# Two score halves of the first attention block held back for VectorE's copies, and a cap of four key tiles on the block behind it

## The chip, the cores and the metric

The kernel runs on one NeuronCore of one Trainium2 chip. The metric is the device time of one execution in microseconds. Before the change it is 1393.85 us, the median of three runs (1393.54 to 1394.19).

## The reference

One layer on 2048 tokens of 512 features, all in float32. Cut to what matters:

```python
xn = _layernorm(x)
# attention, 32 heads of 16
qkv = (xn @ wqkv).reshape(B, S, 3, 32, 16)...
scores = einsum("bhqd,bhkd->bhqk", q, k) * 16 ** -0.5
s = einsum("bhqk,bhkd->bhqd", softmax(scores), v) ... @ wo
# feed-forward of the same xn, hidden width 1792
f = (silu(xn @ w_gate) * (xn @ w_up)) @ w_down
return x + s * silu(f)
```

## The kernel before, in words

**Engines.** PE (TensorE) does every matmul, ACT (ScalarE) the exponentials and the tanh, DVE (VectorE) copies, casts and splits, POOL (GpSimd) a few fills and element-wise products, and SP issues most DMAs. Each engine runs its own instructions in the order in which the program wrote them. They wait for each other by semaphores, when a buffer has to be full or has to be free.

**Stages.** A prologue (up to about 156 us) normalises the tokens and projects queries, keys and values to DRAM. Then comes the attention, with the feed-forward and the output projection dealt out between its matmuls, and a short tail.

**Attention.** Its work is cut into 32 units (8 groups of four heads, times 4 blocks of 512 queries). A unit has 16 key tiles of 128 keys. The key tiles of a unit are grouped into *blocks* of 2 to 6 tiles, written `(k, n)` below: k key tiles, and n slots of other work. `plan()` (L62 to L115) makes the list of blocks. A key tile has two *pairs* of score matmuls (L906), and a pair is two matmuls (h = 0 and 1) which sit in different row groups of the array and run side by side. The pairs of a block are numbered n = 0 to 2k - 1 (the loop at L885). After pair n come `parts[n]` fills (`fill`, L924). A fill is one step of the feed-forward generator `ffn` (L251), which is two matmuls side by side as well (L242). So a pair and a fill cost PE one *slot* each.

**Banks.** Each score half takes one PSUM bank of 512 floats. Even pairs go to the two banks of `score`, and one 1024-wide exponential (L909) empties both. Odd pairs go to `single0` and `single1`, each emptied by a 512-wide exponential (L916). The last pair of a block goes to `single0` and to the bank `spare`. A bank is free for its next pair when its reader has finished. In the rows that follow buffer numbers are mostly left out, so `single` is either of the two.

**Halves kept back.** Where a pair's number stands in the block's `shared` list (L902, L912), one of its halves is not read by ACT: DVE copies it to SBUF (L913), which frees the bank, and ACT does its exponential there in place (L926) when all pairs and fills of the block have been issued. An even pair in that list uses `spare` for its second half.

**Values.** The value matmuls of a block (`values`, L423, matmul L428, all of the array, no fill beside them) are issued inside the next block, ahead of its pair n = 2. So pairs n = 0 and n = 1 of a block run before the values of the block ahead of it.

**What the planner does.** `plan()` fixes the first block by hand (4 tiles, no shared halves, fills from `FIRST`) and searches the rest for the cheapest way through key tiles and fills: each block costs 327 plus terms for bad shapes (L92). Block shapes that stand in `SHARED` have lists made by hand. `FIRST[0]` fills are issued ahead of the first block (L881), and `FIRST[1:]` are the fills behind its eight pairs.

**Other work that the opening carries.** After every 24 fills one hidden tile is complete: ACT does a tanh (`th`, L269), and DVE two products (`ga`, L270 and L271) and splits into a high and a low part (`hh`, L235 and L236). At the first fill of each hidden tile DVE splits the gate and up weights of a later one (`guh` and `gul`, L203 and L204). At the 24th fill of the first tile in the attention and at the 8th fill of the later ones DVE splits a down weight (`wd`, L213 and L214). There is one buffer for the raw down weight (`wdr`), and its next load (L209, on SP) starts when the split has read it. POOL writes rows of ones into two key buffers (L160) shortly after the attention has begun.

Before the change the list of blocks begins (4, 20), (6, 24), (6, 24), with 4 fills ahead of it.

Of the kernel before, what the change touches and what calls it, by code (L numbers as in the profile page):

```python
# [40 lines left out]
LIMIT = 160.0  # L41
SIZES = (2, 3, 4, 5, 6)
LAST = (3, 3, 3, 3, 2, 2)
FIRST = (4, 1, 4, 0, 4, 1, 2, 4, 4)
EARLY = 2


# [14 lines left out]
def plan():  # L62

    ends = [0]
    for i in range(2 * NB):  # L70
        nf = GROUPS[i % 2].stop - GROUPS[i % 2].start
        for n in [3 * DC] * nf + [3 * nf] * NT:
            ends.append(ends[-1] + n)

    ends = [n - ends[1] for n in ends[2:]]
    first = [(4, ends[0])]
    units = H // 4 * NB
    start, stop = sum(k for k, _ in first), (units - 2) * KT
    pace = (ends[-1] - ends[0]) / (stop - start)
    short = lambda k, n: 60 if (k, n) in SHARED else 250 * max(0, 6 * (k - 1) - n)  # L80
    ways = {at: {} for at in range(start, stop + 1)}
    ways[start][ends[0], 4] = 0, None
    for at in range(start, stop):
        room = KT - at % KT
        for (done, last), (cost, _) in ways[at].items():
            rem = next((n for n in ends if n > done), done) - done
            for k in SIZES:
                for n in [rem] + list(range(3, rem - 2)):
                    to = at + k, done + n
                    if not n or n > 6 * k + 6 or k > room or room - k == 1:  # L90
                        continue
                    if abs(to[1] - ends[0] - (to[0] - start) * pace) > 45:  # L92
                        continue
                    c = cost + 327 + short(k, n) + (120 if k == 6 and n < 24 else 0) + (700 if k == last == 6 and n < 24 else 0) + (650 if n == rem and k == 2 else 0) + abs(n - 4.1 * k) / 2
                    if (to[1], k) not in ways[to[0]] or ways[to[0]][to[1], k][0] > c:
                        ways[to[0]][to[1], k] = c, ((at, (done, last)), (k, n))

    rest = [3 * (DT - 1)] * EARLY
    pairs = {4: (2, 2), 5: (3, 2), 6: (3, 3)}
    best = lambda r: min((w[0], key) for key, w in ways[stop - r].items() if key[0] == ends[-1])  # L100
    cost = lambda r: best(r)[0] + sum(short(k, n) for k, n in zip(pairs[r], rest))
    r = min((r for r in pairs if any(done == ends[-1] for done, _ in ways[stop - r])), key=cost)
    middle, step = [], ways[stop - r][best(r)[1]][1]
    while step:
        middle.insert(0, step[1])
        step = ways[step[0][0]][step[0][1]][1]
    rest += [3 * DT] * (NT * (NB - 1))
    parts = []
    for k, n in first + middle + list(zip(pairs[r] + 2 * LAST, rest)):
        m = 2 * k - 2  # L110
        even = [n // m + (i < n % m) for i in range(m)]
        shared, behind = SHARED.get((k, n), ((), even))
        parts.append((k, shared, [0, 0, *behind]))
    parts[0] = 4, (), list(FIRST[1:])
    return parts  # L115


# [1 line left out]
def tile_block(ctx: ExitStack, tc: tile.TileContext, x, wqkv, wo, w_gate, w_up, w_down, out):  # L119
# [356 lines left out]
    def fill(n):  # L476
        nonlocal given
        while n > 0 and not blocked():
            next(queue[0][1])
            queue[0][2] -= 1  # L480
            if not queue[0][2]:
                queue.pop(0)
            n -= 1
            given += 1

    blocks = plan()

    begin, n = [], 0
# [381 lines left out]
    for u in range(units):  # L870
# [3 lines left out]
        for now in range(begin[u], begin[u + 1]):  # L874
# [5 lines left out]
            if not now:  # L880
                fill(FIRST[0])  # L881
            if now < 2:
# [140 lines left out]
```

## Time and profile before

| what | us |
|---|---|
| median of three runs | 1393.85 |
| the profiled execution | 1393.63 |
| its span, first to last instruction | 1391.9 |
| attention's first slot to the fourth block's pair n = 2 | 156.15 to 198.53 |
| PE busy, of the span | 1383.6 |
| ACT busy, of the span | 1155.7 |
| DVE busy, of the span | 772.5 |

The granted TensorE clock is 0.999 over the span. In a timeline a row has the start in us, the duration in us, the engine, the line, the operation with output and inputs, the shape and the number of instructions merged, and in brackets the idle time of the engine ahead of it with what ended it. PEld is PE's loading of weights, which runs ahead of the matmul that uses them, and which waits where the matmul's bank is not free yet.

### The profile page before, as it was taken

The page shows a single profiled execution, that of the slowest core. Times are in us where ns is not written, and L with a number is a line of the kernel's source. Part 1 is how long each engine was busy: PE and PEld are TensorE (multiplying, and loading weights), DVE is VectorE, ACT ScalarE, POOL GpSimd, SP SyncE. Part 2 cuts the span into 40 slices and gives each one's busy share as a digit, 9 for nine tenths or more (in the row PEclk, how much of TensorE's full clock was granted, in tenths as well). Part 3 has the DMA queues.
Part 4 walks back from the last instruction along what each step waited for, and adds up shares of the span by engine and source line. Part 5 has one row for each costly group of instructions (what it writes and reads, how often), then busy time and mean ns, then how long its engine had stood idle before and what let it go on. Part 6 is the DMA issues. An engine that isn't in the chain of part 4 may idle for free.

```text
span 1391.9 us, 27666 instructions
## 1 busy us (share of the span) xinstructions
PE 1383.6 (99%) x11197; PEld 863.9 (62%) x11197; DVE 772.5 (56%) x1242; ACT 1155.7 (83%) x1932; POOL 89.4 (6%) x102
## 2 busy tenths in 40 slices
PE   9999999999999999999999999999999999999998
PEld 7788656556555655665556555666556556655554
DVE  6643466355646664565465643665466445655755
ACT  6733588888989898889998988888989888899874
POOL 4200100000000000000000000000000000000344
PEclk9999999999999999999999999999999999999999
DMA  7778541124463511233723402357323311232543
GB/s 241 263 249 269 141 116 44 35 69 112 98 138 81 134 43 36 50 87 87 170 60 109 114 13 51 74 127 152 84 67 94 99 28 47 73 102 85 190 146 108
DMA packets 128693, 149.21 MB, mean 107 GB/s; under 512 B 12593, under 2 KB 80689, under 8 KB 127790
## 3 DMA queue, kind: packets, MB, share of 16 engines
q1 hardware_dynamic: 123246, 126.72, 35.5%
q0 software_dynamic: 4880, 20.12, 3.9%
q8 instruction: 90, 1.47, 0.5%
q10 hardware_dynamic: 432, 0.52, 0.1%
q14 instruction: 45, 0.37, 0.1%
HBM read 107.46 MB, written 40.11 MB: 106 GB/s over the span
## 4 chain that ended last, share of the span: by engine, by line
PE 86%; DVE 2%; ACT 1%; issue 0%; DVEq 0%
PE acc L428 32%; PE bankx L242 29%; PE score L906 9%; PE single L906 8%; PE banky L242 6%; PE spare L906 1%; ACT pr L916 0%; ACT pr L909 0%; PE spare L961 0%; PE banky L961 0%; DVE pr L913 0%; DVE gul L204 0%; DVE wd L335 0%; DVE wd L334 0%; DVE on L446 0%
## 5 line engine op out<-in xcount | busy, mean ns | idle before, releaser
L428 PE MATMUL acc<-pr,vst 128*17 128x512 f32 x4096 | 460.4, 593 | 0.0
L916 ACT ACTIVATE pr<-single 128x512 f32<-128x512 f32 x759 | 427.7, 605 | 19.9 <-PE spare L906 3.1
L909 ACT ACTIVATE pr<-score 128x1024 f32<-128x1024 f32 x327 | 337.1, 1031 | 90.3 <-PE score L906 86.7
L242 PE MATMUL bankx<-fx,guh 64*128 64x512 f32 x896 | 290.3, 392 | 0.1
L242 PE MATMUL banky<-fx,guh 64*128 64x512 f32 x896 | 290.4, 392 | 0.0
L428 PEld LDWEIGHTS acc<-pr,vst 128*17 128x17 f32 x4096 | 114.9, 97 | 277.9 <-issue 273.6
L913 DVE COPY pr<-spare 128x512 f32<-128x512 f32 x185 | 127.9, 691 | 169.0 <-PE spare L906 156.8
L906 PE MATMUL score<-qst,kst 50*128 50x512 f32 x839 | 218.9, 419 | 0.0
L906 PE MATMUL single<-qst,kst 50*128 50x512 f32 x916 | 212.9, 399 | 0.8 <-DVE pr L913 0.7
L242 PE MATMUL banky<-wd,hh 64*128 64x512 f32 x672 | 196.1, 392 | 0.0
L242 PE MATMUL bankx<-wd,hh 64*128 64x512 f32 x672 | 196.0, 391 | 0.0
L926 ACT ACTIVATE pr<-pr 128x512 f32<-128x512 f32 x342 | 187.2, 641 | 1.3 <-DVE pr L913 1.3
L242 PEld LDWEIGHTS bankx<-fx,guh 64*128 64x128 f32 x896 | 166.8, 186 | 21.3 <-DVEq L815 0.6
L242 PE MATMUL bankx<-fx,gul 64*128 64x512 f32 x448 | 175.8, 392 | 0.0
L242 PE MATMUL banky<-fx,gul 64*128 64x512 f32 x448 | 175.5, 392 | 0.0
L906 PEld LDWEIGHTS score<-qst,kst 50*128 50x128 f32 x839 | 98.2, 184 | 118.4 <-ACT pr L916 77.1
L242 PEld LDWEIGHTS banky<-fx,guh 64*128 64x128 f32 x896 | 166.9, 186 | 2.0
L913 DVE COPY pr<-single 128x512 f32<-128x512 f32 x157 | 108.4, 691 | 64.8 <-PE single L906 36.9
L916 ACT ACTIVATE pr<-score 128x512 f32<-128x512 f32 x185 | 111.4, 602 | 34.9 <-PE spare L906 27.5
L242 PEld LDWEIGHTS bankx<-wd,hh 64*128 64x128 f32 x672 | 125.1, 186 | 18.9
L906 PEld LDWEIGHTS single<-qst,kst 50*128 50x128 f32 x916 | 114.0, 184 | 26.5 <-ACT pr L916 8.3
L242 PEld LDWEIGHTS banky<-wd,hh 64*128 64x128 f32 x672 | 125.1, 186 | 5.2
(179 smaller groups left out, 1680.3 us busy)
## 6 DMA issues: line engine op xcount, KB each, us to landing
gur<-in_B_w_gate_dram SPq DMA_DIRECT2D x56, 256.0 KB
gur<-in_B_w_up_dram SPq DMA_DIRECT2D x56, 256.0 KB
wdr<-in_B_w_down_dram SPq DMA_DIRECT2D x56, 256.0 KB
kst<-k_d SPq DMA_DIRECT2D x192, 64.0 KB
qst<-q_d SPq DMA_DIRECT2D x192, 64.0 KB
fx<-xt_d SPq DMA_DIRECT2D x24, 512.0 KB
q_d<-parts SPq DMA_DIRECT2D x16, 512.0 KB
k_d<-parts SPq DMA_DIRECT2D x16, 512.0 KB
```

The source lines that it names most:

```text
L242: mm(bank, lhs[h], rhs[h], start=start, stop=stop)
L428: mm(acc[h * 32:h * 32 + DH + 1], v[:, kt % CT, h * (DH + 1):(h + 1) * (DH + 1)], probs[2 * i + h // 2][:, h % 2], start=kt == 0, stop=kt ...
L906: mm(banked[h], k[r, j, kc * P:(kc + 1) * P], q[r, j], start=True, stop=True)
L909: exps.append(act(pr, both_banks, AF.Exp, scale=0.25))
L913: dve.tensor_copy(pr[:, h], banked[h])
L916: exps.append(act(pr[:, h], banked[h], AF.Exp, scale=0.25))
L926: exps.append(act(part, part, AF.Exp, scale=0.25))
```

## The change

Three edits, all in `plan()` and its tables. `FIRST` deals the 24 fills of the opening otherwise: 2 in place of 4 ahead of it, and 2, 4, 1, 3, 4, 2, 2, 4 behind its pairs in place of 1, 4, 0, 4, 1, 2, 4, 4. `OPEN` gives the first block a `shared` list of pairs 5 and 7. And a block that follows the first one costs 900 more if it has over four key tiles.

```diff
-FIRST = (4, 1, 4, 0, 4, 1, 2, 4, 4)
+FIRST = (2, 2, 4, 1, 3, 4, 2, 2, 4)
+OPEN = (5, 7)
...
-                    c = cost + 327 + short(k, n) + ... + (700 if k == last == 6 and n < 24 else 0) + (650 if n == rem and k == 2 else 0) + abs(n - 4.1 * k) / 2
+                    c = cost + 327 + short(k, n) + ... + (700 if k == last == 6 and n < 24 else 0) + (900 if at == start and k > 4 else 0) + (650 if n == rem and k == 2 else 0) + abs(n - 4.1 * k) / 2
...
-    parts[0] = 4, (), list(FIRST[1:])
+    parts[0] = 4, OPEN, list(FIRST[1:])
```

The list of blocks then begins (4, 22), (2, 9), (4, 15), (6, 24), with 2 fills ahead of it. From the block that starts at key tile 10 of the first unit on, it is the list of before, block for block, one place later (109 blocks in place of 108). Lines behind the tables have a number higher by one.

What moves on DVE, from the start of the attention on. Before (`gur` are the raw gate and up weights, `pr` a tile of probabilities):

```order
L203 CAST guh<-gur 128x1024
L204 TENSOR_TENSOR gul<-gur,guh 128x1024
L270 SCALAR_TENSOR_TENSOR ga<-th,bankx 128x512
L271 SCALAR_TENSOR_TENSOR ga<-ga,banky 128x512
L235 CAST hh<-ga 128x512
```

And now, at the same place:

```order
L204 CAST guh<-gur 128x1024
L205 TENSOR_TENSOR gul<-gur,guh 128x1024
L914 COPY pr<-single_8968 128x512
L914 COPY pr<-single_8967 128x512
L271 SCALAR_TENSOR_TENSOR ga<-th,bankx 128x512
L272 SCALAR_TENSOR_TENSOR ga<-ga,banky 128x512
L236 CAST hh<-ga 128x512
```

Two copies of score halves now stand ahead of the first hidden tile's products, where there was none.

Further on, on DVE behind the split of the first down weight, before:

```order
L203 CAST guh<-gur 128x1024
L204 TENSOR_TENSOR gul<-gur,guh 128x1024
L913 COPY pr<-spare 128x512
L213 CAST wd<-wdr 128x512
L214 TENSOR_TENSOR wd<-wdr,wd 128x512
L913 COPY pr<-spare 128x512
L913 COPY pr<-single_8968 128x512
L913 COPY pr<-spare 128x512
L913 COPY pr<-single_8968 128x512
L270 SCALAR_TENSOR_TENSOR ga<-th,bankx 128x512
```

And now:

```order
L204 CAST guh<-gur 128x1024
L205 TENSOR_TENSOR gul<-gur,guh 128x1024
L214 CAST wd<-wdr 128x512
L215 TENSOR_TENSOR wd<-wdr,wd 128x512
L914 COPY pr<-spare 128x512
L914 COPY pr<-single_8968 128x512
L914 COPY pr<-single_8967 128x512
L271 SCALAR_TENSOR_TENSOR ga<-th,bankx 128x512
```

The five copies of the old second block are gone from among the weight splits. The second block has none now, and the three copies here are those of the new third block, all behind the split of the second down weight.

On ACT, from the opening block's pair n = 4 on, before (`score` is the pair of banks that one exponential empties):

```order
L909 ACTIVATE pr<-score_8966 128x1024
L916 ACTIVATE pr<-single_8967 128x512
L916 ACTIVATE pr<-single_8968 128x512
L909 ACTIVATE pr<-score_8966 128x1024
L916 ACTIVATE pr<-single_8967 128x512
L916 ACTIVATE pr<-spare 128x512
L269 ACTIVATE th<-bankx 128x512
L909 ACTIVATE pr<-score_8966 128x1024
```

And now, from the same pair on:

```order
L910 ACTIVATE pr<-score_8966 128x1024
L917 ACTIVATE pr<-single_8967 128x512
L910 ACTIVATE pr<-score_8966 128x1024
L917 ACTIVATE pr<-spare 128x512
L270 ACTIVATE th<-bankx 128x512
L927 ACTIVATE pr<-pr 128x512 x2
L910 ACTIVATE pr<-score_8966 128x1024
```

Two of ACT's exponentials out of PSUM became two in SBUF, and stand behind the tanh, still ahead of the second block's first one. On SP the DMAs stand in the order of before.

More of the change, by code (lines that the diff above doesn't have):

```diff
@@ L93, in plan @@
                         continue
-                    c = cost + 327 + short(k, n) + (120 if k == 6 and n < 24 else 0) + (700 if k == last == 6 and n < 24 else 0) + (650 if n == rem and k == 2 else 0) + abs(n - 4.1 * k) / 2
+                    c = cost + 327 + short(k, n) + (120 if k == 6 and n < 24 else 0) + (700 if k == last == 6 and n < 24 else 0) + (900 if at == start and k > 4 else 0) + (650 if n == rem and k == 2 else 0) + abs(n - 4.1 * k) / 2
                     if (to[1], k) not in ways[to[0]] or ways[to[0]][to[1], k][0] > c:
```

## The prediction, made before the changed kernel was run

> **What bounds the kernel now.** I read the page's first part, then the opening by stages.
>
> ```profile
> PE 1383.6 (99%) x11197; PEld 863.9 (62%) x11197; DVE 772.5 (56%) x1242; ACT 1155.7 (83%) x1932; POOL 89.4 (6%) x102
> ```
>
> PE is busy for 99% of the span, ACT for 83%. So only time that PE loses can be won. The change reaches the first ten key tiles, and from there on the list of blocks is the old one. So I cut the stretch from the first slot (156.15) to the fourth block's pair n = 2 (198.53) where the value matmuls begin and end. Columns: length, then busy time (instructions) of PE, PEld, DVE, ACT and POOL, the clock, DMA.
>
> ```profile
> 156.15:165.54 9.39, 9.39 (x69) 6.84 (x69) 1.44 (x2) 8.35 (x14) 3.78 (x4) 1.00 0.75 173
> 165.54:169.10 3.56, 3.56 (x35) 0.84 (x34) 3.01 (x6) 2.21 (x4) 0.00 (x0) 1.00 0.02 5
> 169.10:179.16 10.06, 9.31 (x77) 7.22 (x73) 7.67 (x12) 7.87 (x14) 0.00 (x0) 1.00 0.57 146
> 179.16:184.43 5.27, 5.27 (x50) 1.39 (x48) 4.32 (x6) 4.97 (x10) 0.00 (x0) 1.00 0.72 178
> 184.43:193.26 8.83, 8.83 (x76) 7.58 (x73) 4.48 (x7) 7.87 (x14) 0.00 (x0) 1.00 0.47 105
> 193.26:198.53 5.27, 5.27 (x50) 1.39 (x48) 4.54 (x7) 4.97 (x10) 0.00 (x0) 1.00 0.02 4
> ```
>
> The rows are: slots of block 0 (and n = 0, 1 of block 1), its values, slots of block 1, its values, slots of block 2, its values; 42.38 us together. What these slots cost without a wait is read from the same shapes later:
>
> ```profile
> 285.16:293.83 8.67, 8.67 (x76) 7.02 (x73) 3.41 (x5) 7.78 (x14) 0.00 (x0) 1.00 0.33 77
> 293.83:299.11 5.28, 5.28 (x52) 1.39 (x50) 4.32 (x6) 4.98 (x10) 0.00 (x0) 1.00 0.00 0
> 1279.67:1285.21 5.54, 5.54 (x50) 4.21 (x46) 2.44 (x4) 4.80 (x9) 0.00 (x0) 1.00 0.26 74
> 1288.77:1291.99 3.22, 3.22 (x30) 2.38 (x27) 1.04 (x2) 2.39 (x5) 0.54 (x1) 1.00 0.97 354
> 1291.99:1293.83 1.84, 1.84 (x18) 0.37 (x17) 1.70 (x4) 1.84 (x3) 0.00 (x0) 1.00 1.03 383
> ```
>
> They are a (6, 24) block, its values, a (4, 15) block, a (2, 9) block, its values; four tiles' values take 3.56, as above. Block 1, a (6, 24), takes 10.06 against 8.67, so it loses **1.39**; block 2 loses **0.16**. Block 0 has 8 pairs, 24 fills and two pairs of block 1, 34 slots. The first score pair, and the first and the last start of four undisturbed slots:
>
> ```profile
> 157.15 0.44 PE L906 MATMUL score<-qst,kst 50*128 50x512 f32 x2
> ...
> 162.88 0.39 PE L242 MATMUL banky<-fx,guh 64*128 64x512 f32 x1
> ...
> 163.81 0.40 PE L906 MATMUL spare<-qst,kst 50*128 50x512 f32 x1
> ```
>
> From 162.88 to 163.81, four slots in 0.93 make 0.2335 each, and 34 make 7.94, with 0.10 ahead of the values 8.04. Block 0 takes 9.39, so it loses **1.35**. Where these losses are, PEld's timeline shows, by who ended its wait:
>
> ```profile
> 159.23 0.18 PEld L906 LDWEIGHTS single<-qst,kst 50*128 50x128 f32 x1 [0.30 <-ACT pr L916]
> 162.54 0.19 PEld L906 LDWEIGHTS score<-qst,kst 50*128 50x128 f32 x2 [0.39 <-ACT pr L909]
> 173.19 0.18 PEld L906 LDWEIGHTS spare<-qst,kst 50*128 50x128 f32 x1 [0.55 <-DVE pr L913]
> 175.46 0.18 PEld L906 LDWEIGHTS spare<-qst,kst 50*128 50x128 f32 x1 [1.05 <-issue]
> ```
>
> In block 0 the banks come back late from ACT. In block 1 they come back late from DVE's copies of `spare`, 0.55 and 1.05 (the row names the issue, but a copy that is shown below ends at 175.39, just ahead of it). The Trainium skill (Trainium Kernel Development and Optimization, Performance Expectations) holds matmul busy time for a bad measure, since matmuls are pipelined, and takes LDWEIGHTS instead. By PE's busy time the six windows hide no more than 0.75 (10.06 less 9.31), and the sum below would be a gain of at most 0.75. By the spacing of the slots they hide 2.90. The trace sides with the page: the rows of PEld show waits in the first window, where PE counts as busy throughout.
>
> **Block 0.** The two halves kept back are two DVE copies, and two exponentials that read SBUF in place of PSUM. Their prices, and ACT's queue in the opening:
>
> ```profile
> L916 ACT ACTIVATE pr<-single 128x512 f32<-128x512 f32 x759 | 427.7, 605 | 19.9 <-PE spare L906 3.1
> L926 ACT ACTIVATE pr<-pr 128x512 f32<-128x512 f32 x342 | 187.2, 641 | 1.3 <-DVE pr L913 1.3
> 157.67 1.03 ACT L909 ACTIVATE pr<-score 128x1024 f32<-128x1024 f32 x1 [1.04 <-DVE gul L204]
> 158.59 1.08 ACT L916 ACTIVATE pr<-single 128x512 f32<-128x512 f32 x2
> 159.55 1.04 ACT L909 ACTIVATE pr<-score 128x1024 f32<-128x1024 f32 x1
> ...
> 166.60 1.15 ACT L916 ACTIVATE pr<-single 128x512 f32<-128x512 f32 x2
> 169.64 1.03 ACT L909 ACTIVATE pr<-score 128x1024 f32<-128x1024 f32 x1 [1.89 <-PE score L906]
> ```
>
> ACT starts 0.52 after the first score pair (157.15), and then runs without a break until 167.75: 0.92 for a full pair, 0.96 for two halves. Then it sits idle for 1.89 while PE does the values. The halves kept back move 2 x 0.5 us from the full stretch into this idle time, and cost there 2 x 0.04 more than out of PSUM.
>
> The walk: with 2 fills ahead, n = 0 goes to PE at 156.15 + 0.53 = 156.68, its exponential runs from 157.20 to 158.23, those of n = 1 end at 158.72 and 159.20. PE wants n = 3 ten slots after n = 0, at 159.02: its second bank is free at 159.24, a wait of 0.23. n = 4 would go at 160.0; the exponential of n = 2 (159.09 to 160.12) frees it at 160.17 with the release, a wait of 0.12 with what the first left. n = 5 wants the banks of n = 3 (free at 161.1) at 161.35; n = 6 those of n = 4 (162.05) at 162.05; n = 7 half of n = 5 (162.5) at 162.75, and `spare`, which nobody used. Block 1's n = 1 wants DVE's copy of n = 7 (163.9) at 164.15. So 0.33 of 1.35 stays, and the values begin at 164.5: **gain 1.02**. The same walk over the list of before puts them at 165.50, where the trace has 165.54. The bounds: 1.35 (no wait left) and, where copies and exponentials run later than walked, nothing or a loss (rival B).
>
> The copies cost nothing by this: DVE is idle ahead of 165.88 for 8.26, and two copies of 0.69 take 1.38 of it.
>
> ```profile
> 165.88 0.69 DVE L270 SCALAR_TENSOR_TENSOR ga<-th,bankx 128x512 f32<-128x512 f32 x1 [8.26 <-ACT th L269]
> 169.98 0.69 DVE L214 TENSOR_TENSOR wd<-wdr,wd 128x512 fp32r<-128x512 f32 x1
> 170.70 0.36 SPq L209 DMA_DIRECT2D wdr<-in_B_w_down_dram x1
> 172.45 0.68 DVE L913 COPY pr<-spare 128x512 f32<-128x512 f32 x1
> 173.64 0.43 DVE L213 CAST wd<-wdr 128x512 fp32r<-128x512 f32 x1 [0.50 <-DMA wdr<-in_B_w_down_dram]
> 174.71 0.68 DVE L913 COPY pr<-spare 128x512 f32<-128x512 f32 x1
> ```
>
> **Blocks 1 and 2.** From 165.88 on DVE works off the first hidden tile and the weight splits, without a break until 173.1. The copies of the old block 1 queue behind that, and then behind the second down weight, whose load leaves SP at 170.70 and lands at 173.64, 2.94 later. The new block 1 has no copies, so nothing that PE needs stands behind the splits: its cost is that of the (2, 9) block above, and the loss of **1.39** goes. What is late next is block 2's copy of n = 2. The tanh comes 1.0 earlier, so the first down weight is split by 169.65, the second one lands at about 172.6 and is split by 173.75, and the copy can begin with its score, done at about 173.75. It ends at 174.45, and PE wants `spare` again for n = 7, at about 177.0: **2.5 us of slack**. The three halves of block 2 kept back cost ACT 3 x 0.64 beside 3.56 of values. The (6, 24) behind it is the old block 2; I take its **0.16** for a rest of the same backlog, which goes too.
>
> The price of one more block: from the windows, (2, 9) and (4, 15) take 3.22 + 1.84 + 5.54 + 3.56 = 14.16, the (6, 24) in whose place they stand 8.67 + 5.28 = 13.95, so **0.21** more. Score, value and fill matmuls are as many as before. DMAs stand in their old order on SP; keys and queries are loaded well ahead.
>
> **Sum:** -1.02 - 1.39 - 0.16 + 0.21 = -2.36. The profiled execution takes 1393.63 (1.73 more than its span), and would take 1391.27. It is 0.22 under the median, so 1393.85 - 2.36 = 1391.49.
>
> **Rivals.**
>
> A, the forecast: 1391.2 to 1391.8.
>
> B, GpSimd holds the copies up. The new copies meet POOL's four fills, and a DVE operation next to POOL has taken longer elsewhere:
>
> ```profile
> 34.98 1.30 POOL L555 TENSOR_TENSOR wl<-wraw,wh 128x512 fp32r<-128x512 f32 x1 [1.98 <-ACT wh L551]
> 35.02 1.54 DVE L611 TENSOR_SCALAR xn<-facc,mv,rs 128x512 f32<-128x512 f32 x1
> 45.63 3.90 POOL L160 MEMSET kst<- 2x1024 f32 x4
> 45.65 0.69 DVE L702 TENSOR_TENSOR parts<-ps,parts 128x512 fp32r<-128x512 f32 x1 [0.84 <-ACT parts L701]
> 160.74 3.94 POOL L160 MEMSET kst<- 2x1024 f32 x4 [11.33 <-ACT pr L909]
> ```
>
> The scaling out of SBUF took 1.54 beside a POOL subtraction of 1.30. A DVE subtraction out of PSUM took 0.69 beside the same four fills, and the copies out of PSUM above take 0.68 each. If each new copy waits out one fill (0.98), block 1's n = 1 goes 0.4 later: 1391.9. If both wait for the last fill (164.7), its bank is free at 165.4 and block 0 loses 2.0 more: 1393.5. The Trainium skill (SBUF — State Buffer, Who interferes with whom) calls the port pair that VectorE and GpSimd share an exclusive lock: whoever comes second blocks fully. It exempts operations with one SBUF input at most outside the two-port modes, and the subtraction's 0.69 agrees; no row shows a copy out of PSUM beside POOL.
>
> C, the change does half of what it says: block 1's loss comes back in the two short blocks, because DVE is busy there for 7.67 (window 169.10:179.16) where the (2, 9) and (4, 15) windows had 1.04 and 2.44. Without 1.39 of the gain: 1392.9. Against it stands the slack of 2.5.
>
> D, slower. Block 2's only use of `spare` ahead of n = 7 stands on DVE behind the split of the second down weight. A landing later than 2.94 + 2.5 = 5.4 after its issue delays PE one to one; from 7.8 on the kernel is slower than before, and at 11 it is 0.2% slower (1397). The row shows 2.94, and the old block 1 felt only 0.50 of it.
>
> E, more than forecast: block 0 without any wait, and runs at the low end (they spread by 0.3 around the median): 1390.9.
>
> **How the numbers follow.** A measurement of this kernel can tell about 0.2% from no change, which is 2.8 us: faster means under 1391.06. Chances: A 0.76, B 0.08 (0.05 and 0.03), C 0.07, D 0.03, E 0.06. So the likeliest is faster by 0.17%, within that bound. E and a little of A make faster 0.07, D's far end slower 0.02, the rest 0.91. The range takes in A, B's near case, C and E: 1390.9 to 1392.9.
>
> **What would show it.** The first value matmul at about 164.5; block 0's values follow at once with no wait for the two late exponentials; slots of about 3.2 and 5.5 in blocks 1 and 2; the (6, 24) block's pair n = 2 at about 182.2 in place of 184.43; copies of 0.69 beside the fills. Wrong are the steps if a copy takes over 1 us (B), or if PEld waits for DVE in block 1 or 2 (C, D).

## The result: 1.90 us faster, 0.14%, and the profile after

The changed kernel takes 1391.99 us, the median of 22 runs (1391.70 to 1392.22). The kernel before, run beside it, takes 1393.89 (22 runs, 1393.28 to 1394.67). The ratio is 0.9987, with a 95% interval of 0.9981 to 0.9993. That is a gain of 1.90 us. It lies inside the 0.2% that the prediction counts as no change, though the interval lies clear of 1, and it is 0.46 less than the 2.36 of the forecast. The profiled execution takes 1391.74, its span is 1389.9. This is the engines' line of its page:

```profile
PE 1382.6 (99%) x11197; PEld 867.1 (62%) x11197; DVE 772.6 (56%) x1242; ACT 1155.8 (83%) x1930; POOL 89.6 (6%) x102
```

The instructions are the old ones, but for two of ACT's (1930 in place of 1932). The windows of the opening, cut as before where the value matmuls begin and end (length, then PE, PEld, DVE, ACT, POOL, clock, DMA):

```profile
155.84:164.65 8.81, 8.81 (x68) 6.70 (x68) 2.56 (x3) 7.66 (x12) 3.79 (x4) 1.00 0.77 183
164.65:168.21 3.56, 3.56 (x35) 0.84 (x33) 3.12 (x6) 3.16 (x6) 0.00 (x0) 1.00 0.02 7
168.21:171.43 3.22, 3.22 (x31) 2.37 (x27) 3.15 (x5) 2.24 (x4) 0.00 (x0) 1.00 0.22 50
171.43:173.27 1.84, 1.84 (x19) 0.36 (x18) 0.68 (x3) 1.84 (x3) 0.00 (x0) 1.00 0.70 224
173.27:178.87 5.60, 5.60 (x51) 4.67 (x47) 2.54 (x4) 4.79 (x9) 0.00 (x0) 1.00 0.85 200
178.87:182.43 3.56, 3.56 (x35) 0.88 (x34) 3.10 (x5) 3.56 (x7) 0.00 (x0) 1.00 0.63 137
182.43:191.25 8.82, 8.82 (x77) 7.97 (x73) 5.71 (x8) 7.99 (x15) 0.00 (x0) 1.00 0.56 130
191.25:196.52 5.27, 5.27 (x50) 1.39 (x48) 4.54 (x7) 4.97 (x10) 0.00 (x0) 1.00 0.02 4
```

Together they take 40.68 us where the six windows of before took 42.38: a gain of **1.70**. Term by term, against the forecast:

| term | forecast | measured | from |
|---|---|---|---|
| block 0 | -1.02 | -0.58 | 9.39 to 8.81 |
| block 1's loss and the new boundary | -1.39 + 0.21 | -1.11 | 10.06 + 5.27 to 3.22 + 1.84 + 5.60 + 3.56 |
| the (6, 24) block behind | -0.16 | -0.01 | 8.83 to 8.82 |
| sum | -2.36 | -1.70 | |

The rest of the attention, from there to the end of the span, takes 1193.4 both times (1391.9 - 198.53 and 1389.9 - 196.52). The profiled execution was also 0.31 earlier at the first slot (155.84 in place of 156.15). Nothing ahead of that slot was changed, and the profiles below begin the attention anywhere from 156.0 to 156.5, so I put no weight on it. Between 1.70 in the profile and 1.90 in the medians stand 0.20 us. The other kernels have such differences on either side (a table stands behind the experiments).

What became of the waits in block 0 shows in PEld's timeline, with the first score pair on PE:

```profile
155.81 0.18 PEld L243 LDWEIGHTS bankx<-fx,guh 64*128 64x128 f32 x1 [0.55 <-DVE guh L204]
156.39 0.48 PEld L907 LDWEIGHTS score<-qst,kst 50*128 50x128 f32 x2 [0.25 <-issue]
156.42 0.77 PE L907 MATMUL score<-qst,kst 50*128 50x512 f32 x2
159.32 0.18 PEld L907 LDWEIGHTS single<-qst,kst 50*128 50x128 f32 x1 [0.30 <-ACT pr L917]
```

The first pair is new in this list. Its two weight loads take 0.48 together, where two that run side by side take 0.19: the trace's records have its halves at 156.416 and 156.718, so the second one is **0.30 late**. The waits on ACT that the walk had left are there as well: 0.30 at pair n = 3 (159.32) where it had 0.23, and 0.16 at n = 4 (160.24) where it had 0.12. One of 0.19 at n = 6 (162.14) it had not. No wait on DVE is left in blocks 1 and 2, where before had 0.55 and 1.05.

ACT's queue and the engines around it:

```profile
157.27 1.02 ACT L910 ACTIVATE pr<-score 128x1024 f32<-128x1024 f32 x1 [0.95 <-PE score L907]
160.36 3.96 POOL L161 MEMSET kst<- 2x1024 f32 x4 [11.24 <-ACT pr L910]
161.98 0.69 DVE L914 COPY pr<-single 128x512 f32<-128x512 f32 x1 [4.96 <-PE single L907]
163.37 0.69 DVE L914 COPY pr<-single 128x512 f32<-128x512 f32 x1 [0.69 <-PE spare L907]
164.78 1.14 ACT L927 ACTIVATE pr<-pr 128x512 f32<-128x512 f32 x2
168.75 1.03 ACT L910 ACTIVATE pr<-score 128x1024 f32<-128x1024 f32 x1 [0.94 <-PE score L907]
172.58 0.43 DVE L214 CAST wd<-wdr 128x512 fp32r<-128x512 f32 x1 [1.12 <-DMA wdr<-in_B_w_down_dram]
173.83 0.69 DVE L914 COPY pr<-spare 128x512 f32<-128x512 f32 x1
177.15 0.39 PE L907 MATMUL spare<-qst,kst 50*128 50x512 f32 x1
```

Both new copies take 0.69 beside POOL's four fills (160.36 to 164.32). The two exponentials kept back run beside the value matmuls, 164.78 to 165.92, and ACT's idle time there falls from 1.89 to 0.94. The copy in block 2 frees `spare` at 174.52, and PE uses it at 177.15: a slack of 2.63.

### The profile page after: what moved, and what is told of

The parts are those of the page before. It is cut to its first block, busy times and chain, and to the rows that moved or that the text cites. A ratio compares the mean times of both kernels' runs of the same rounds, so it can differ in the third digit from the quotient of the medians.

```text
span 1389.9 us, 27664 instructions
## 1 busy us (share of the span) xinstructions
PE 1382.6 (99%) x11197; PEld 867.1 (62%) x11197; DVE 772.6 (56%) x1242; ACT 1155.8 (83%) x1930; POOL 89.6 (6%) x102
## 4 chain that ended last, share of the span: by engine, by line
PE 88%; DVE 1%; issue 0%; DVEq 0%
PE acc L429 32%; PE bankx L243 29%; PE score L907 10%; PE single L907 8%; PE banky L243 7%; PE spare L907 1%; PE spare L962 0%; PE banky L962 0%; DVE wd L336 0%; DVE pr L914 0%; DVE wd L335 0%; DVE on L447 0%; DVE o L454 0%; PE score L962 0%; DVE o L434 0%; DVE y L969 0%
```

## Experiments

All are judged by the profile's windows first, since half a microsecond is 0.04% of the time. "Opening" is the sum of the windows from the first slot to the end of the values of the block that ends at key tile 16: 42.38 before, 40.68 after.

### The parts apart

**Fill list and copies without the cap.**

```diff
-                    c = cost + 327 + ... + (900 if at == start and k > 4 else 0) + ...
+                    c = cost + 327 + ... + ...
```

> The change without the cap: the opening has its new fills and its two halves kept back, and the list of blocks goes on (6, 24), (6, 24) as before. Theory (the opening and the cap act apart; the second block loses its time to copies that queue on VectorE behind the weight splits): the first block's slots take about 8.8 us as in the changed kernel, the second block's about 10.1 as before, and the kernel is 0.5 to 0.6 us faster than before. Rival (it is enough that VectorE's backlog begins earlier): the second block's slots come down to 9.3 or less, and the kernel is at least 1.3 us faster than before.

It took 1393.04 (11 runs; before beside it 1393.77, ratio 0.9994, 0.9985 to 1.0003). Block 0 and block 1:

```profile
156.05:164.88 8.83, 8.83 (x69) 6.60 (x69) 2.80 (x4) 7.66 (x12) 3.78 (x4) 1.00 0.80 183
...
168.43:178.44 10.01, 9.25 (x76) 7.10 (x72) 7.49 (x12) 7.86 (x14) 0.00 (x0) 1.00 0.59 147
```

Block 0 has nearly its whole gain without the cap (0.56 of 0.58), and block 1, a (6, 24) again, nearly its whole loss: 10.01 against 8.67.

```profile
172.34 0.18 PEld L907 LDWEIGHTS spare<-qst,kst 50*128 50x128 f32 x1 [0.34 <-DVE pr L914]
174.74 0.18 PEld L907 LDWEIGHTS spare<-qst,kst 50*128 50x128 f32 x1 [1.17 <-issue]
```

These are the waits of before, 0.55 and 1.05, with the sum near the same (1.51 and 1.60). The DVE copy that the second one waits for runs from 173.99 to 174.67, behind the split of the second down weight. So a block 0 that is 0.6 shorter doesn't help block 1, and the cap is worth its 1.1 by itself.

**The cap alone.**

```diff
-FIRST = (2, 2, 4, 1, 3, 4, 2, 2, 4)
-OPEN = (5, 7)
+FIRST = (4, 1, 4, 0, 4, 1, 2, 4, 4)
+OPEN = ()
```

> The cap alone: fills of the opening and its empty list as before, then (2, 9), (4, 15), (6, 24). Theory (the copies leave VectorE's backlog, whenever that begins): the first block's slots take 9.4 us as before, the second block's 3.2, the third block's 5.6 with no wait for VectorE, and the kernel is 1.0 to 1.3 us faster than before. Rival (the short blocks are free of waits only because the tanh comes earlier with the new opening): second and third block together lose 0.5 us or more, and the kernel is at most 0.6 us faster than before.

It took 1392.61 (before 1393.77, ratio 0.9991, 0.9982 to 1.0000). Its block 0 is that of before, and the opening takes 41.25, which is 1.13 less:

```profile
156.15:165.53 9.38, 9.38 (x69) 6.82 (x69) 1.40 (x2) 8.34 (x14) 3.78 (x4) 1.00 0.77 173
```

**The fill list without the copies, and the copies without the fill list** (the cap in both):

```diff
-OPEN = (5, 7)
+OPEN = ()
```

> The change with an empty list of shared halves in the opening: new fills and cap, ScalarE reads all halves out of PSUM. Theory (most of the first block's gain is the even deal of the fills with ScalarE's earlier start, the copies only spare the wait at the second block's pair n = 1): the first block's slots take about 9.1 to 9.2 us, 0.35 more than in the changed kernel, and the kernel is about 1.5 us faster than before. Rival (the copies carry the first block's gain): its slots take 9.4 or more, and the kernel is 1.3 us faster than before or less.

```diff
-FIRST = (2, 2, 4, 1, 3, 4, 2, 2, 4)
+FIRST = (4, 1, 4, 0, 4, 1, 2, 4, 4)
```

> The change with the old fills: the halves of pairs 5 and 7 are kept back, the cap stands, the fills are dealt out as before (4 ahead, then 1, 4, 0, 4, 1, 2, 4, 4). Theory (with those fills TensorE stands at pairs n = 3, 5 and 6 for banks that ScalarE has to free, and the copies come too late to help): the first block's slots take 9.3 to 9.4 us as with the cap alone, and the kernel is 1.0 to 1.3 us faster than before. Rival (the copies help by themselves): the slots take 9.1 us or less, and the kernel is 1.4 us faster than before or more.

Without the copies the time is 1392.46 (before 1393.77, ratio 0.9991, 0.9982 to 1.0000), with the copies and the old fills 1392.73 (before 1393.88, ratio 0.9991, 0.9982 to 1.0000). Block 0 in the first:

```profile
156.17:165.26 9.09, 9.09 (x68) 6.69 (x68) 1.23 (x1) 8.16 (x14) 3.78 (x4) 1.00 0.77 179
```

And in the second, with two of the waits of its PEld:

```profile
156.02:165.42 9.40, 9.40 (x69) 6.82 (x69) 2.59 (x3) 7.78 (x12) 3.79 (x4) 1.00 0.74 174
```

```profile
159.59 0.18 PEld L907 LDWEIGHTS single<-qst,kst 50*128 50x128 f32 x1 [0.30 <-ACT pr L917]
162.41 0.19 PEld L907 LDWEIGHTS score<-qst,kst 50*128 50x128 f32 x2 [0.39 <-ACT pr L910]
```

So the fill list alone gives 0.30 of block 0's 0.58, the copies behind it give the other 0.28, and the copies alone give nothing (9.40 against 9.39). With the old fills the last wait (162.41) is that of pair n = 6, twelve slots ahead of the values, for the banks that the exponential of n = 4 frees. The first half that is kept back is one of n = 5, behind that exponential, so what ACT saves comes too late.

### Where block 1's loss came from

**The kernel before, with a buffer of its own for the second down weight**, so that its load doesn't wait for the split of the first. `on` are the tiles for the attention's outputs, and `on[3]` holds nothing yet.

```diff
-        raw = one.tile([P, D], F32, tag="wdr", name="wdr")
+        raw = on[3] if i == 1 else one.tile([P, D], F32, tag="wdr", name="wdr")
```

> The kernel before, with the second down weight of the attention loaded into a tile that is idle there, so that its load does not wait for the split of the first one; nothing else is changed. Theory (the second block's longer wait is VectorE's: its copy stands behind the split of that weight, which waits 0.50 us for the landing): that wait of VectorE goes, the second block's slots take 9.5 to 9.7 us in place of 10.06, and the kernel is 0.4 to 0.5 us faster. Rival (TensorE waits there for the semaphores of newly loaded keys, of which the eighth pair of that block is the first reader): the second block's slots stay at 10.0 us and the time at that of before.

It took 1393.45 (before 1393.88, ratio 0.9996, 0.9987 to 1.0005). Block 1 takes 9.47 in place of 10.06:

```profile
169.44:178.91 9.47, 9.32 (x76) 7.22 (x72) 7.59 (x12) 7.87 (x14) 0.00 (x0) 1.00 0.77 178
```

```profile
173.40 0.42 DVE L213 CAST wd<-on 128x512 fp32r<-128x512 f32 x1
173.54 0.18 PEld L906 LDWEIGHTS spare<-qst,kst 50*128 50x128 f32 x1 [0.54 <-DVE pr L913]
174.47 0.68 DVE L913 COPY pr<-spare 128x512 f32<-128x512 f32 x1
175.22 0.18 PEld L906 LDWEIGHTS spare<-qst,kst 50*128 50x128 f32 x1 [0.45 <-issue]
```

The split starts without a wait now, and PE's second wait falls from 1.05 to 0.45, while the first stays at 0.54. So DVE's queue is what block 1 lost its time to: 0.6 of it to the landing of the weight, and the rest, by the rows, to the work ahead of the copies. That is the mechanism that the prediction named. The edit also moves the loads that stand behind this one on SP: those of the keys of tiles 12 to 15 leave at 164.51 in place of 171.11. No pair of block 1 reads these keys.

### Why block 0 gave less

In the changed kernel the first score pair waits for 11 semaphores with its first half and for 5 more with its second. These are the waits as they stand in the program:

```
L907 MATMUL score_8966<-qst_556,kst_548 128x512 [waits DMAHW2_49,DMAHW1_49,DMAHW3_49,DMAHW0_49,DMAHW4_49,DVE_49,DMAHW5_49,PE_49,DMAHW6_49,Activation_49,Pool_49]
L907 MATMUL score_8966<-qst_556,kst_548 128x512 [waits DMAHW5_49,DMAHW4_49,DMAHW7_49,DMAHW3_49,Pool_49]
```

PE's sequencer has a record of its own for every two of them, and the last one of each half (Pool) is waited for by the half's weight load. In the trace the records lie 0.106 apart: 155.884, 155.990, 156.096, 156.201 and 156.307, then the first weight load at 156.386; 156.506 and 156.611, then the second at 156.687. The semaphores of the second half had their last updates by 154.20, so its two records wait for nothing. The Trainium skill (Perfetto Trace Analysis, Identifying Dependency Chains) says that instructions which wait on several engines may get extra semaphore instructions ahead of them; the trace agrees, and has the 0.106 for each, which the page doesn't give. In the kernel before, the seven records lie from 156.19 to 156.85, all beside four fills, and delay nothing. Behind two fills the last of them is not covered.

**No fill ahead of the first pair.**

```diff
-FIRST = (2, 2, 4, 1, 3, 4, 2, 2, 4)
+FIRST = (0, 4, 4, 1, 3, 4, 2, 2, 4)
```

> The change with no fill ahead of the first score pair (the two fills go behind pair n = 0: 4 there). Theory (the first score pair has 16 semaphores to wait for, and TensorE's sequencer takes them one after another, for about 0.85 us from the start of the attention, whatever the fills): the first pair starts at 0.55 to 0.6 and 0.85 to 0.9 us after the point where the first fill would have, TensorE has nothing else to do meanwhile, the first block's slots take about 9.3 us, and the kernel is about 1.4 us faster than before, 0.5 less than the changed kernel. Rival (the pair goes as soon as the queue ahead is empty, as my walk had it): ScalarE starts 0.47 us earlier, the first block's slots take about 8.3 us, and the kernel is about 2.4 us faster than before.

It took 1392.62 (before 1393.77, ratio 0.9990, 0.9981 to 0.9999). The first window is cut from the last matmul of the prologue to the first value matmul:

```profile
155.71:165.40 9.69, 8.97 (x71) 6.67 (x69) 3.20 (x4) 7.87 (x12) 3.78 (x4) 1.00 0.42 118
```

```profile
156.79 0.41 PEld L907 LDWEIGHTS score<-qst,kst 50*128 50x128 f32 x2 [1.13 <-issue]
```

The pair goes no earlier without the two fills: its halves start 1.12 and 1.35 after the last matmul of the prologue (1.12 and 1.42 in the changed kernel). So it isn't the two fills that set its start, and without them PE has nothing to do until the pair goes: the values begin 9.69 behind that matmul, in place of 9.36. The rival, that the pair moves up with the fills gone, falls. That the semaphores hold the first half is not shown by this run, though. Their records lie 0.106 apart here too (156.294 to 156.717, then the weight load at 156.793), but one of them is for ACT's last copy of the prologue, which ends at 156.72, so the half could hardly have gone earlier without the others. A run below tells the two apart.

**The fills dealt out with four ahead, and other pairs kept back.**

```diff
-FIRST = (2, 2, 4, 1, 3, 4, 2, 2, 4)
-OPEN = (5, 7)
+FIRST = (4, 3, 3, 2, 3, 1, 2, 2, 4)
+OPEN = (3, 4, 7)
```

> The changed kernel with 4 fills ahead, fills 3, 3, 2, 3, 1, 2, 2, 4 behind the pairs, and halves of pairs 3, 4 and 7 kept back. Theory (block 0 loses what its banks come back late from ScalarE and what the first pair's semaphores take; with 4 fills ahead those are taken beside the fills, and with a half of pairs 3 and 4 read by VectorE no bank is late): both halves of the first pair start side by side 1.0 us after the first fill, the first block's slots take 8.0 to 8.2 us against 8.8 in the changed kernel, and the kernel is 2.4 to 2.7 us faster than before. Rival (three late exponentials and a copy out of the spare bank make the values or the last pair wait): slots and values of the first block together gain less than 0.3 us on the changed kernel, and the kernel is about 2 us faster than before.

It took 1391.65 (11 runs, 1391.27 to 1391.96; before 1393.88, ratio 0.9983, 0.9974 to 0.9992), and its opening 40.09, which is 0.59 less than that of the changed kernel. Nearly all of that is block 0 (8.81 to 8.24):

```profile
156.47:164.71 8.24, 8.24 (x68) 6.83 (x69) 3.29 (x4) 7.11 (x12) 2.76 (x3) 1.00 0.71 171
```

```profile
157.24 0.22 PEld L907 LDWEIGHTS score<-qst,kst 50*128 50x128 f32 x2
162.15 0.19 PEld L907 LDWEIGHTS score<-qst,kst 50*128 50x128 f32 x2 [0.16 <-ACT pr L917]
```

The halves of the first pair lie side by side again, with no wait. The small waits left on ACT cost 0.20 (8.24 against 8.04 for 34 slots without one). Its opening is shorter than those of before and after. The step is below what the medians of different runs can tell apart, so its 0.59 is read from the windows.

**Fewer semaphores for the first pair.** Two kernels, both without the branch for large scores, in which the first queries and keys would be loaded again: this takes the first pair's waits from 11 and 5 to 6 and 4. What the kernel does for inputs with large scores is left out with it. The data here never takes that branch.

```diff
-        with tc.If(fast < 1):
-            with tc.tile_pool(name="gen", bufs=1) as gen:
...
-                load_q(0)
-                load_shift(0)
```

> The changed kernel without its branch for large scores (which this data never takes). Left out with it: what the kernel would do for inputs whose scores are too large. The first score pair then waits for 6 and 4 semaphores in place of 11 and 5. Theory (PE's sequencer takes these waits one after another, 0.106 us for each record, and two fills don't cover them): the first half goes on time, the second half 0.1 to 0.25 us behind it in place of 0.30, and block 0's slots take 8.55 to 8.75 us in place of 8.81. Rival (the walk misses something else of block 0, such as the banks' way back): 8.78 to 8.85.

The second one has, besides, two small matmuls in the prologue that read the same keys and queries (their result is read by nobody). They take over the waits for the loads, and the first pair waits for one semaphore, ACT's, with its first half, and for none with its second.

```diff
+                if not more and n == 10:
+                    ahead = pps.tile([P, 512], F32, tag="ps", name="ahead")
+                    for h, to in enumerate((ahead, extra)):
+                        r = slice(h * HALF, h * HALF + NROW)
+                        mm(to[:, :16], kst[0][r, 0, :P], qst[0][r, 0, :16], start=True, stop=True)
```

> The kernel of the run before this one, and two matmuls of 16 columns in the prologue that read the first keys and queries into banks nobody reads, so that the semaphores of these loads are waited for there; the first score pair then waits for one semaphore, and its second half for none. Theory: the two halves go within 0.06 us of each other, 0.50 to 0.57 us behind the first fill, and block 0's slots take 8.35 to 8.55 us; the walk of the prediction had 8.37. Rival (something else of block 0 was walked wrongly): the halves side by side and still 8.75 to 8.85.

They took 1392.45 and 1392.02 (one run of each; before beside them 1394.19). Without the branch, from the first slot and from the last matmul of the prologue:

```profile
156.18:165.13 8.95, 8.89 (x69) 6.69 (x69) 1.38 (x2) 7.77 (x12) 2.84 (x3) 1.00 0.64 156
155.85:165.13 9.28, 9.22 (x70) 6.70 (x69) 1.38 (x2) 7.77 (x12) 2.84 (x3) 1.00 0.62 150
```

With the waits in the prologue as well:

```profile
156.02:164.83 8.81, 8.80 (x69) 6.31 (x69) 1.38 (x2) 7.77 (x12) 3.78 (x4) 1.00 0.77 174
155.69:164.83 9.14, 9.13 (x70) 6.31 (x69) 1.38 (x2) 7.77 (x12) 3.78 (x4) 1.00 0.74 167
```

And its timeline: the last prologue matmul, the first fills (one of the two banks of each), the first pair, and ACT's last copy and first exponential:

```profile
155.69 0.40 PE L651 MATMUL extra<-vl,xt 128*128 128x512 f32 x1
156.02 0.49 PE L243 MATMUL bankx<-fx,guh 64*128 64x512 f32 x1
156.13 0.59 ACT L728 COPY vt<-extra 128x512 f32<-128x512 f32 x1 [2.21 <-PE extra L651]
156.36 0.39 PE L243 MATMUL bankx<-fx,guh 64*128 64x512 f32 x1
156.76 0.19 PEld L880 LDWEIGHTS score<-qst,kst 50*128 50x128 f32 x2 [0.45 <-ACT vt L728]
156.77 0.51 PE L880 MATMUL score<-qst,kst 50*128 50x512 f32 x2
157.11 0.39 PE L243 MATMUL bankx<-fx,gul 64*128 64x512 f32 x1
157.44 1.03 ACT L883 ACTIVATE pr<-score 128x1024 f32<-128x1024 f32 x1 [0.72 <-PE score L880]
```

The halves came closer as the theory said: 0.23 apart, then 0.01, in place of 0.30. But both numbers for block 0 missed. By the window from the first fill nothing was gained: 8.81 in the second kernel is the rival's own number, and 8.95 in the first lies above both ranges. The reason is in the rows. Without the branch the first fill goes 0.33 after the prologue's last matmul, no longer 0.55, where it had waited for DVE's `guh`. The pair does not move with it: with one semaphore left it waits for ACT's last copy of the prologue, and goes 0.04 behind its end. That copy is a floor that my theory had not seen. So the first fill is no common mark for these kernels, and the last matmul of the prologue was taken as one after these runs. Counted from the prologue's last matmul they are (us; the copy of ACT ends 1.02 or 1.03 behind it in all):

| kernel | first pair's halves | ACT's first exponential | first value matmul | from exponential to values |
|---|---|---|---|---|
| before | 1.54, 1.58 | 2.07 | 9.93 | 7.87 |
| after | 1.12, 1.42 | 1.97 | 9.36 | 7.38 |
| no branch | 1.12, 1.35 | 1.90 | 9.28 | 7.38 |
| waits in the prologue | 1.07, 1.08 | 1.75 | 9.14 | 7.39 |
| no fill ahead | 1.12, 1.35 | 1.91 | 9.69 | 7.79 |
| four ahead, pairs 3, 4, 7 | 1.54, 1.59 | 2.06 | 8.78 | 6.72 |

The three kernels with the fill list and copies of the change have the same 7.38 behind the first exponential. So a first exponential that starts earlier brings the values forward one to one, and with the pair's semaphores gone the first exponential comes 1.97 - 1.75 = **0.22** earlier.

Their price in the changed kernel is a little higher. ACT's sequencer has such records too, 0.077 apart (156.134, 156.211 and 156.288 in this last run). In the other kernels of the table the record that waits for PE is ACT's last: it ends at 157.225 in the changed kernel, and the exponential starts 0.045 behind it. In this run it ends at 157.319, one more record stands behind it, and the exponential starts 0.121 behind its end. That is 0.08 which came with the two matmuls: without the branch alone it was 0.046. Counted from the prologue's last matmul, that record ends at 1.93 in the changed kernel and at 1.63 here, so the semaphores cost **0.30**. That 0.30 is an estimate from these records; 0.22 is what the run won.

### The last 0.15

**A small matmul that reads the keys of tiles 12 to 15 early**, ahead of pair n = 2 of the (6, 24) block (its result is read by nobody). Pair n = 4 there is the first to read them, and waits for 5 and 4 semaphores.

```diff
+                if n == 2 and now == 3:
+                    r = slice(HALF, HALF + NROW)
+                    mm(spare[:, :16], kst[3][r, 0, :P], q[r, 0, :16], start=True, stop=True)
```

> The changed kernel with one small score matmul more (16 columns, into the spare bank, result unused), issued behind the third block's values and ahead of the (6, 24) block's pair n = 2. It reads the second half of the key chunk that this block's pair n = 4 is the first to read, and so takes 4 of the 9 semaphores that this pair waits for while TensorE still works off the values. Theory (the 0.16 us that this block loses, before and after the change, are TensorE's sequencer taking the semaphores of newly loaded keys): the second half of pair n = 4 goes beside the first, and the block's slots take 8.65 to 8.75 us in place of 8.82, the small matmul included. Rival (a bank or the keys themselves come late): the second half stays 0.15 us or more behind the first, and the slots take 8.8 to 8.9 us. The whole time moves by too little to tell from no change.

One run took 1391.92 (before 1394.35). Pair n = 4 in the changed kernel, and then here, with the block's window:

```profile
184.06 0.18 PEld L907 LDWEIGHTS score<-qst,kst 50*128 50x128 f32 x1 [0.17 <-issue]
184.29 0.18 PEld L907 LDWEIGHTS spare<-qst,kst 50*128 50x128 f32 x1
```

```profile
184.42 0.18 PEld L910 LDWEIGHTS score<-qst,kst 50*128 50x128 f32 x1 [0.15 <-ACT pr L913]
184.43 0.18 PEld L910 LDWEIGHTS spare<-qst,kst 50*128 50x128 f32 x1
```

```profile
182.70:191.44 8.74, 8.74 (x77) 7.62 (x73) 5.71 (x8) 7.92 (x15) 0.00 (x0) 1.00 0.55 135
```

The weight loads of the halves go 0.01 apart in place of 0.23, and the block takes 8.74 in place of 8.82, though it has a matmul more. So at least half of the 0.15 above 8.67 is in the semaphores of freshly loaded keys. It isn't the keys themselves that come late: with the second down weight's own buffer their loads leave SP 6.6 earlier (164.51 for 171.11), and the block still takes 8.82. The first half now meets a wait of 0.15 for ACT. Whether the rest of the 0.15 would go without the added matmul is open.

### Windows against medians

| kernel | opening, change | median, change |
|---|---|---|
| after | -1.70 | -1.90 |
| no cap | -0.62 | -0.73 |
| cap alone | -1.13 | -1.16 |
| no copies | -1.42 | -1.31 |
| no fill ahead, from the prologue's last matmul | -1.35 | -1.15 |
| four ahead, pairs 3, 4, 7 | -2.29 | -2.23 |
| old fills, copies, cap | -1.13 | -1.15 |
| second down weight | -0.59 | -0.43 |

The two agree within 0.2, with either sign. So the 0.20 of the changed kernel is the size of what these medians differ by anyway; its cause is open. It also means that the expectations for the whole time were narrower than the medians can tell. Four of them missed: no cap 0.73 for 0.5 to 0.6, no copies 1.31 for 1.5, no fill ahead 1.15 for 1.4, four ahead 2.23 for 2.4 to 2.7. Of the windows, those with four ahead (8.24 for 8.0 to 8.2) and with the second down weight (9.47 for 9.5 to 9.7) missed by 0.04 and 0.03.

## Why the prediction was right, and where its steps were off

**Right: a small gain, and which part of the change carries most.** The median came out at 1391.99 against 1391.5, inside the range, though 0.2 above the 1391.8 at which the forecast's own case ended. That the range holds it is in part luck: it went up to 1392.9 for rivals B and C, and neither happened. The time is close to B's near case (1391.9), but no copy was held up. One sign also looks better than it is: the first value matmul came at 164.65 for a forecast of 164.5, but 0.31 of that is the earlier start of the profiled execution.

- *Block 1's loss of 1.39 goes, for 0.21 of boundary.* Forecast 1.18, measured 1.11 in the profile and 1.13 with the cap alone. The cause named, copies behind DVE's weight splits, is borne out by the second down weight's own buffer (10.06 to 9.47). The slots of 3.22 are those read from a far later block; 5.60 is 0.06 above the 5.54 read there, which is most of the 0.07 that is missing, and its cause was not looked for.
- *2.5 us of slack for block 2's copy.* It was 2.63, and the down weight's load landed 2.96 after its issue (169.62 on SP). So rivals C and D had no hold: no wait of PEld in blocks 1 and 2 is put down to DVE. Rival E is out as well: block 0 still loses 0.77 (8.81 against 8.04).
- *The copies cost nothing beside POOL.* They took 0.69, so rival B is out. The rule of the Trainium skill (SBUF — State Buffer, Who interferes with whom), that an operation with one SBUF input at most stays clear of GpSimd outside the two-port modes, now has a row for a copy out of PSUM, and the trace agrees: 0.69 beside the fills, 0.68 to 0.69 elsewhere.

**Off: "With 2 fills ahead, n = 0 goes to PE at 156.15 + 0.53 = 156.68, its exponential runs from 157.20".** Counted from the last prologue matmul this put the exponential at 1.60 and the values at 8.92; they came at 1.97 and 9.36. The 0.44 splits by the runs above. 0.30 is the semaphores of the first pair (0.22 won back by the run without them, 0.08 more by the records), above all those of its second half. The walk had no term for them, since in the trace of before four fills cover them. With the semaphores gone the pair starts as walked (1.07 against 1.08), but ACT's record that waits for it ends 0.55 behind its start, where it took 0.48 in before: that is 0.07. In that run the slots that follow a wait take 0.34 (156.02 to 156.36, 156.77 to 157.11), where the walk took the distance from a pair behind four fills; why they are that long is open. The last 0.07 is the walk itself, 7.38 from exponential to values against 7.32.

**Off: "I take its 0.16 for a rest of the same backlog, which goes too".** The (6, 24) block took 8.81 to 8.83 in before, after and in every kernel that left it alone, whatever stood ahead of it. At least half of it is a property of its own place, the first use of new keys (8.74 with their semaphores taken earlier). The size was small, but the step had no row behind it, only the nearness of another loss.

## What to carry to other kernels

A list that is tuned to where a bank comes free must also be checked against the first instruction that needs freshly loaded data: it may have many semaphores to wait for (16 for the first pair here), and the work ahead of it in the queue is what hides them. Take that work away and they show. When parts of a schedule are compared, count from an event that none of them moves; here the first slot moved, and only the prologue's last matmul showed the effect.

## What the runs showed of the hardware that was not expected

- Semaphores that are long done still cost PE's sequencer 0.106 us for each extra record: seven records for a pair with 16 semaphores. Behind two fills the pair's second half went 0.30 us late, and a kernel without these semaphores won 0.22 us back; behind four fills the halves lie 0.04 apart.
- ACT's sequencer has such records as well, 0.077 us apart. One that stands behind the record which waits for PE put the first exponential 0.121 us behind the end of that wait, in place of 0.045.
- A busy PE is not evidence against such a loss: PE counts 8.81 of 8.81 us busy in the window that holds it.
- A slot of PE that follows a wait took 0.34 us in one kernel (156.02 and 156.77), and the first slot of the attention 0.31 in before and after, against 0.2335 in the steady stream.
